# A gated layer whose matmuls use the two 64-row halves of the array side by side

## The chip, the cores and the metric

One core of a Trainium2 chip runs the whole kernel. The metric is the device time of one execution in microseconds (us). A difference is told from no change where it is over about 0.2%.

## The reference, cut to what matters

An mLSTM attention (4 batches, 8 heads, 768 positions, head size 40) gives 3072 rows of 320 numbers. Each row goes to one of eight experts (320 to 1024, relu, back to 320, times the row's routing weight). The last part is a gated layer, with 1536 hidden features:

```python
def _moe2_ref(x, w_gate, w_val, w_out):      # x [3072, 320]; w_gate, w_val [320, 1536]; w_out [1536, 320]
    gate = 1.0 / (1.0 + np.exp(-(x @ w_gate)))
    val = x @ w_val
    return (gate * val @ w_out).astype(np.float32)
```

## The kernel before

The kernel runs three stages after one another: attention, experts, gated layer. The order of instructions on each engine is the order in which the code issues them.

**Numbers in two parts.** Every operand of the experts and of the gated layer is held as a high and a low part (`split`, `f64_split`), both of the type float32r. A product is three matmuls into one bank of the accumulation memory: high by high, high by low, low by high.

**The gated layer** works on 6 groups of 512 rows (`NG`) by 12 blocks of 128 hidden features (`NF2`): 72 steps, numbered `t`, with `g = t // 12` and `f = t % 12`. In step `t`:

- `gated_l1(t)` takes two of the banks 0, 1, 2, 6 for gate and value and calls `l1_tile` (lines 922 to 926) for each. The 320 inputs are 128 + 128 + 64. The first two parts take three matmuls each. For the last 64, the weights' high and low parts stand under one another in one 128-row tile (`wgs`, `wvs`), the input stands in both halves of its own tile, and two matmuls give all four products. That is 8 matmuls of 512 columns for the gate and 8 for the value.
- then ScalarE takes the sigmoid (line 1527), VectorE multiplies (1528), ScalarE copies the high part `hh` (1530) and POOL subtracts for the low part `hl` (1532; in the last step VectorE does).
- `gated_l2(t - 2)` multiplies the features made two steps before by `w_out`: for each of 4 blocks of 128 rows three matmuls of 320 columns (lines 1544 to 1546), added up in banks 3, 4, 5, 7 over the 12 steps of a group.
- after the twelfth, `gated_out` copies the four banks (ScalarE line 1556, VectorE line 1558), and POOL issues an indirect DMA for each (1560).
- `piece()` prepares the next piece of weights: `f64_split` turns 64-bit inputs into the two parts with VectorE bit operations (lines 1076, 1079, 1082, then 1086, 1089 and the low part 1071) with one ScalarE relu (1085) in between and one ScalarE copy (1068). In the steps 0 to 11 these are the 12 pieces of `w_out`; those of `w_gate` and `w_val` are prepared during the experts, four of them for the last 64 rows, which write `wgs` and `wvs` with two low operations and two copies each. `defer` is a list of small operations on routing flags, of which eight are left when the gated layer starts; one of them is a matmul (line 1208).

In the experts, each hidden block has a low part `hl` made by VectorE (line 1015), which stands in VectorE's queue among the operations of the pieces, and which the matmuls of line 936 need.

**Elsewhere in the kernel**, the first attention tile multiplies 40-row operands that stand in the rows 0 to 39 and 64 to 103 (line 429; later tiles use all 128 rows), and line 476 writes 40-column results in two column halves.

Of the kernel before, what the change touches and what calls it, by code (L numbers as in the profile page):

```python
# [9 lines left out]
F32 = mybir.dt.float32  # L10
# [12 lines left out]
def kernel(  # L23
# [15 lines left out]
    nc = tc.nc  # L39
# [33 lines left out]
    def next_bank(banks, name):  # L73
        t = turn.get(banks, 0)
        turn[banks] = t + 1
        return bank(banks[t % len(banks)], name)
# [839 lines left out]
    def l1_tile(ps, ws, xt, f):  # L916

        hi, lo, st = ws
        h, l = xt
        fs = slice(f * P, (f + 1) * P)  # L920
        for kk in range(2):
            nc.tensor.matmul(ps, hi[:, kk, fs], h[:, kk], start=(kk == 0), stop=False)  # L922
            nc.tensor.matmul(ps, hi[:, kk, fs], l[:, kk], start=False, stop=False)  # L923
            nc.tensor.matmul(ps, lo[:, kk, fs], h[:, kk], start=False, stop=False)  # L924
        nc.tensor.matmul(ps, st[:, fs], h[:, 2], start=False, stop=False)  # L925
        nc.tensor.matmul(ps, st[:, fs], l[:, 2], start=False, stop=True)  # L926

    def ring(tag):
        return mw.tile([P, NM], F32R, tag=tag, name=tag, bufs=3)
# [481 lines left out]
    for nm in ("wg", "wv"):  # L1411
        glu[nm] = (
            gp.tile([P, 2, F2], F32R, name=nm + "h"),
            gp.tile([P, 2, F2], F32R, name=nm + "l"),
            gp.tile([P, F2], F32R, name=nm + "s"),
        )

    def whole(t):
        return t

    def glu_piece(nm, kk, c0, n):
        cs = slice(c0, c0 + n)
        if kk < 2:
            src = (w_gate if nm == "wg" else w_val)[:, cs].bitcast(I32)
            hi, lo, st = glu[nm]
            t = f64_load([(slice(0, P), src[kk * P:(kk + 1) * P])], n)
            return lambda: f64_split(t, n, [(whole, hi[:, kk, cs])], [(whole, lo[:, kk, cs])])

        halves = [slice(u * RM, (u + 1) * RM) for u in range(2)]
        t = f64_load(  # L1430
            [(r, w[:, cs].bitcast(I32)[2 * P:DM]) for r, w in zip(halves, (w_gate, w_val))], n
        )

        def parts(u):
            return [
                (lambda z, r=r: z[r], glu[m][2][halves[u], cs]) for r, m in zip(halves, ("wg", "wv"))
            ]

        return lambda: f64_split(t, n, parts(0), parts(1))


    todo = sorted(
# [75 lines left out]
        piece_load()  # L1518
    hs, os_ = {}, {}

    def gated_l1(t):
        g, f = t // NF2, t % NF2
        pg, pv = (next_bank((0, 1, 2, 6), nm) for nm in ("g_ps", "v_ps"))
        l1_tile(pg, glu["wg"], xg[g], f)
        l1_tile(pv, glu["wv"], xg[g], f)
        s = mw.tile([P, NM], F32, tag="sgm", bufs=2, name="sgm")
        nc.scalar.activation(out=s, in_=pg, func=AF.Sigmoid)  # L1527
        nc.vector.tensor_tensor(out=s, in0=pv, in1=s, op=ALU.mult)  # L1528
        gh, gl = ring("hh"), ring("hl")
        nc.scalar.copy(gh, s)  # L1530
        e = nc.gpsimd if t < last else nc.vector
        e.tensor_tensor(out=gl, in0=s, in1=gh, op=ALU.subtract)  # L1532
        hs[t] = (gh, gl)

    def gated_l2(t, js):
        g, f = t // NF2, t % NF2
        if f == 0:
            os_[g] = [bank(j, "o_ps") for j in (3, 4, 5, 7)]
        gh, gl = hs[t]
        wh, wl = wo[f]  # L1540
        for j in js:
            o = os_[g][j][:, 0:DM]
            ts_ = slice(j * P, (j + 1) * P)
            nc.tensor.matmul(o, gh[:, ts_], wh, start=(f == 0), stop=False)  # L1544
            nc.tensor.matmul(o, gh[:, ts_], wl, start=False, stop=False)  # L1545
            nc.tensor.matmul(o, gl[:, ts_], wh, start=False, stop=(f == NF2 - 1))  # L1546
# [19 lines left out]
            puts.append(put)  # L1566

    allj = range(G4)
    for t in range(NG * NF2):
        g, f = t // NF2, t % NF2  # L1570
        piece_due(t)
        gated_l1(t)
        if t >= 2:
            gated_l2(t - 2, allj)
            if (t - 2) % NF2 == NF2 - 1:
                gated_out(g - 1, allj)
        weave(defer[0:4], *piece())
        del defer[0:4]
        if g + 1 < NG and f in (4, 6, 8):
            group_x(g + 1, f // 2 - 2)  # L1580
    for j in allj:
# [188 lines left out]

    NSB = NE * NTILE

    def more_blocks(fp):
        gw = fp.tile([P, NTILE], F32, name="gw")
        for op in soft_ops(fp, gw, raw, ssq):
# [51 lines left out]
        with tc.For_i(0, NE, 1) as e:  # L1827
# [6 lines left out]
            with tc.If(high > low):  # L1834
# [7 lines left out]
                with tc.For_i(low, high, 1) as j:  # L1842
# [35 lines left out]
                    gl = fp.tile([P, NF2, P], F32R, name="fgl")  # L1878
                    for f in range(NF2):
                        pg = mm_ps("fg_ps")[:, 0:P]  # L1880
                        l1_tile(pg, glu["wg"], (yh, yl), f)
                        pv = mm_ps("fv_ps")[:, 0:P]
                        l1_tile(pv, glu["wv"], (yh, yl), f)
                        s = fp.tile([P, P], F32, tag="f_s", name="f_s")
                        nc.scalar.activation(out=s, in_=pg, func=AF.Sigmoid)
                        nc.vector.tensor_tensor(out=s, in0=pv, in1=s, op=ALU.mult)
                        split(gh[:, f], gl[:, f], s)
# [67 lines left out]
```

## Time and profile before

| | us |
|---|---|
| median of 3 runs | 780.74 (780.58 to 780.76) |
| the profiled execution | 783.19 |
| its span, from first to last instruction | 781.5 |
| TensorE matmul busy in the span | 742.0 (95%) |
| VectorE, ScalarE, POOL busy | 408.5, 339.4, 398.8 |

The span is what the trace covers; 1.7 us of the profiled execution lie around it. Busy times are shares of the whole span, and a busy TensorE means that some matmul was in flight, each of which lasts longer than the time to the next one's start. So the time that one matmul costs is read from starts, not from durations. The mean granted TensorE clock was 0.978.

### The profile page before, as it was taken

Reading aid. Unit: us, or ns where it says so; the run is one execution under the profiler, and the core shown is the slowest. Engines: PE = TensorE matmul, PEld = TensorE weight load, DVE = VectorE, ACT = ScalarE, POOL = GpSimd, SP = SyncE. Lnnn points to the kernel's source line nnn. Section 1 sums busy time; section 2 is a strip of 40 time slices with the busy share of each in tenths; the row PEclk is TensorE's granted clock in tenths of the full one; section 3 lists DMA queues with packets and bytes.
Section 4 is the critical chain, followed back from the end, with each engine's and each line's share of the span. In section 5 each row is a group of like instructions: output and inputs, shape, how many; then the busy total and the mean of one; then the engine's idle time right before and its main releaser. Section 6 shows DMA issues by size and latency. Waiting matters only on the chain.

```text
span 781.5 us, 13677 instructions
## 1 busy us (share of the span) xinstructions
PE 742.0 (95%) x5013; PEld 669.1 (86%) x5013; DVE 408.5 (52%) x858; ACT 339.4 (43%) x689; POOL 398.8 (51%) x449
## 2 busy tenths in 40 slices
PE   6789998999999999999999999999999999999995
PEld 5689997998778889998888888888888888888885
DVE  6888888777679889999676611111111111111111
ACT  5765554544866566765444422222222222222221
POOL 6677776647577668786323243342324324324222
PEclk9999999589999999999999999999999999999998
DMA  7555764444445566654022110000000000000001
GB/s 240 172 152 158 237 190 153 138 116 142 153 138 171 156 183 194 183 181 125 21 69 68 34 35 1 1 29 5 1 1 34 0 1 34 1 1 34 1 1 37
DMA packets 39846, 70.19 MB, mean 90 GB/s; under 512 B 4818, under 2 KB 28460, under 8 KB 39772
## 3 DMA queue, kind: packets, MB, share of 16 engines
q1 hardware_dynamic: 36764, 59.61, 25.5%
q0 software_dynamic: 3008, 9.64, 3.9%
q8 instruction: 41, 0.67, 0.3%
q14 instruction: 33, 0.27, 0.1%
HBM read 60.55 MB, written 8.68 MB: 89 GB/s over the span
## 4 chain that ended last, share of the span: by engine, by line
PE 61%; DVE 15%; issue 4%; ACT 1%; DMA 1%; POOL 1%; POOLq 0%; DVEq 0%; ACTq 0%
PE o_ps L1546 5%; PE o_ps L1545 5%; PE o_ps L1544 5%; PE g_ps L922 4%; PE g_ps L923 4%; PE g_ps L924 4%; PE v_ps L923 4%; PE v_ps L922 4%; PE v_ps L924 4%; DVE hl L1015 3%; PE v_ps L926 2%; PE v_ps L925 2%; PE g_ps L925 2%; PE g_ps L926 2%; DVE fa L1089 2%
## 5 line engine op out<-in xcount | busy, mean ns | idle before, releaser
L1532 POOL TENSOR_TENSOR hl<-sgm,hh 128x512 fp32r<-128x512 f32 x71 | 91.9, 1295 | 245.2 <-ACT hh L1530 245.1
L1528 DVE TENSOR_TENSOR sgm<-v_ps,sgm 128x512 f32<-128x512 f32 x72 | 49.8, 691 | 280.6 <-PE v_ps L926 275.2
L1530 ACT CAST hh<-sgm 128x512 fp32r<-128x512 f32 x72 | 44.7, 621 | 136.1 <-DVE sgm L1528 136.1
L1527 ACT ACTIVATE sgm<-g_ps 128x512 f32<-128x512 f32 x72 | 43.0, 597 | 122.6 <-PE g_ps L926 122.5
L1546 PE MATMUL o_ps<-wo,hl 128*128 128x320 f32 x288 | 89.0, 309 | 0.0
L1545 PE MATMUL o_ps<-wo,hh 128*128 128x320 f32 x288 | 88.9, 309 | 0.0
L1544 PE MATMUL o_ps<-wo,hh 128*128 128x320 f32 x288 | 88.6, 308 | 0.0
L429 PE MATMUL s_ps<-qk 128*128 128x128 f32 (+1 forms) x384 | 53.3, 300 | 5.9 <-DMA qk<-in_qkt_dram 5.3
L1544 PEld LDWEIGHTS o_ps<-wo,hh 128*128 128x128 f32 x288 | 54.1, 188 | 2.7
L1545 PEld LDWEIGHTS o_ps<-wo,hh 128*128 128x128 f32 x288 | 54.1, 188 | 2.7
L234 POOL TENSOR_TENSOR w2l<-w2raw,w2h 128x512 fp32r<-128x512 f32 x28 | 39.5, 1409 | 33.2 <-ACT w2h L232 20.9
L936 PE MATMUL y_ps<-hl,w2h 128*128 128x256 f32 (+7 forms) x144 | 49.7, 345 | 5.5 <-DVE hl L1015 5.3
L429 PEld LDWEIGHTS s_ps<-qk 128*128 128x128 f32 (+1 forms) x384 | 48.5, 209 | 7.2 <-DMA qk<-in_qkt_dram 4.8
L1546 PEld LDWEIGHTS o_ps<-wo,hl 128*128 128x128 f32 x288 | 54.1, 188 | 0.0
L223 POOL TENSOR_TENSOR w1l<-w1raw,w1h 128x512 fp32r<-128x512 f32 x32 | 46.2, 1443 | 10.2 <-ACT w1h L220 8.8
L922 PE MATMUL h_ps<-xh,w1h 128*128 128x256 f32 (+7 forms) x144 | 51.2, 356 | 0.0
L935 PE MATMUL y_ps<-hh,w2h 128*128 128x256 f32 (+7 forms) x144 | 50.2, 349 | 0.0
L924 PE MATMUL h_ps<-xh,w1l 128*128 128x256 f32 (+7 forms) x144 | 49.5, 344 | 0.0
L923 PE MATMUL h_ps<-xl,w1h 128*128 128x256 f32 (+7 forms) x144 | 49.4, 343 | 0.0
L1014 ACT ACTIVATE hh<-h_ps 128x256 fp32r<-128x256 f32 (+7 forms) x72 | 34.9, 487 | 32.7 <-PE h_ps L926 28.6
L937 PE MATMUL y_ps<-hh,w2l 128*128 128x256 f32 (+7 forms) x144 | 48.7, 339 | 0.0
L1015 DVE SCALAR_TENSOR_TENSOR hl<-h_ps,hh 128x256 fp32r<-128x256 f32 (+7 forms) x72 | 39.3, 548 | 13.0 <-ACT hh L1014 12.3
(334 smaller groups left out, 2086.4 us busy)
## 6 DMA issues: line engine op xcount, KB each, us to landing
kv<-in_kvo_dram SPq DMA_DIRECT2D x24, 484.0 KB
w2raw<-in_moe_w_dram SPq DMA_DIRECT2D x32, 320.0 KB
w1raw<-in_moe_w_dram SPq DMA_DIRECT2D x32, 256.0 KB
qk<-in_qkt_dram SPq DMA_DIRECT2D x48, 160.0 KB
xs<-x SPq DMA_DIRECT2D x24, 192.0 KB
w1raw<-in_moe_w_dram SPq DMA_DIRECT2D x64, 64.0 KB
raw<-in_moe_w_out_dram SPq DMA_DIRECT2D x12, 320.0 KB
raw<-in_moe_w_gate_dram SPq DMA_DIRECT2D x8, 384.0 KB
```

What stands on the lines that cost most here:

```text
L429: nc.tensor.matmul(pss[u][:, pr_ * L:(pr_ + 1) * L], qk[i % NQ][rows, 2 * u, pr_, :], qk[i % NQ][rows, 1, pr_, :], start=True, stop=True,)
L922: nc.tensor.matmul(ps, hi[:, kk, fs], h[:, kk], start=(kk == 0), stop=False)
L923: nc.tensor.matmul(ps, hi[:, kk, fs], l[:, kk], start=False, stop=False)
L924: nc.tensor.matmul(ps, lo[:, kk, fs], h[:, kk], start=False, stop=False)
L935: nc.tensor.matmul(ys[d], wh, hh, start=first, stop=False)
L936: nc.tensor.matmul(ys[d], wh, hl, start=False, stop=False)
L1015: nc.vector.scalar_tensor_tensor(out=h[f][1], in0=ps, scalar=0.0, in1=h[f][0], op0=ALU.max, op1=ALU.subtract)
L1528: nc.vector.tensor_tensor(out=s, in0=pv, in1=s, op=ALU.mult)
L1532: e.tensor_tensor(out=gl, in0=s, in1=gh, op=ALU.subtract)
L1544: nc.tensor.matmul(o, gh[:, ts_], wh, start=(f == 0), stop=False)
L1545: nc.tensor.matmul(o, gh[:, ts_], wl, start=False, stop=False)
L1546: nc.tensor.matmul(o, gl[:, ts_], wh, start=False, stop=(f == NF2 - 1))
```

## The change

The gated layer issues each matmul as two, on the rows 0 to 63 and 64 to 127 of the operands, and alternates them. In the first phase (`gated_a`) the upper half works on the gate and the lower half on the value: first the last 64 inputs, whose weights now stand as gate in rows 0 to 63 and value in rows 64 to 127 of two tiles `tails` (high, low), then the two blocks of 128, of which each half takes its own 64 rows. In the second phase (`gated_b`) the halves change banks and take the rows that are left. A one-element VectorE write (`seen`) waits for the last matmul of the first phase, and the first matmul of the second phase waits for that write. `gated_l2h` does the same with pairs of output blocks. The product of low by low parts, which the stacked tile had made for the last 64 inputs, is left out. On TensorE a step is `gated_a(t)`, `gated_l2h(t - 2, 0)`, `gated_b(t)`, `gated_l2h(t - 2, 1)`; at the start `gated_a(0)` and `gated_a(1)` come first. The steps 70 and 71 keep the old second layer. The pieces' operations are issued at other places of a step, and the low part `hl` after the output copies and DMAs.

```diff
...
+    tails = [gp.tile([P, F2], F32R, name="wt" + v) for v in "hl"]
...
     def glu_piece(nm, kk, c0, n):
         cs = slice(c0, c0 + n)
         if kk < 2:
             src = (w_gate if nm == "wg" else w_val)[:, cs].bitcast(I32)
-            hi, lo, st = glu[nm]
+            hi, lo = glu[nm]
             t = f64_load([(slice(0, P), src[kk * P:(kk + 1) * P])], n)
             return lambda: f64_split(t, n, [(whole, hi[:, kk, cs])], [(whole, lo[:, kk, cs])])
 
-        halves = [slice(u * RM, (u + 1) * RM) for u in range(2)]
         t = f64_load(
             [(r, w[:, cs].bitcast(I32)[2 * P:DM]) for r, w in zip(halves, (w_gate, w_val))], n
         )
-
-        def parts(u):
-            return [
-                (lambda z, r=r: z[r], glu[m][2][halves[u], cs]) for r, m in zip(halves, ("wg", "wv"))
-            ]
-
-        return lambda: f64_split(t, n, parts(0), parts(1))
+        return lambda: f64_split(t, n, [(whole, tails[0][:, cs])], [(whole, tails[1][:, cs])])
 
 
     todo = sorted(
...
+    gv = {}
+    gate_val = (glu["wg"], glu["wv"])
+
+    def products(rows, ps, w, x, kk, fs, start=False, stop=False):
+        (wh, wl), (h, l) = w, x
+        at = lambda z: z[rows, kk, fs] if len(z.shape) == 3 else z[rows, fs]
+        return [
+            lambda: nc.tensor.matmul(ps, at(wh), h[rows, kk], start=start, stop=False),
+            lambda: nc.tensor.matmul(ps, at(wh), l[rows, kk], start=False, stop=False),
+            lambda: nc.tensor.matmul(ps, at(wl), h[rows, kk], start=False, stop=stop),
+        ]
+
+    seen = const.tile([1, 1], F32, name="seen")
+    sync = mybir.DependencyInfo(mybir.DependencyClass.Sync, mybir.DependencyReason.DATA)
+    passed = {}
+
+    def woven(*chains):
+        return [op() for ops in zip(*chains) for op in ops]
+
+    def note(ins, key):
+
+        passed[key] = nc.vector.memset(seen, 0.0)
+        tc.add_manual_dep(passed[key].ins, ins.ins.name, sync, reason="these products are done")
+
+    def turn_rows(ins, key):
+
+        tc.add_manual_dep(ins.ins, passed.pop(key).ins.name, sync, reason="the other rows wrote the bank")
+
+    def gated_a(t):
         g, f = t // NF2, t % NF2
-        pg, pv = (next_bank((0, 1, 2, 6), nm) for nm in ("g_ps", "v_ps"))
-        l1_tile(pg, glu["wg"], xg[g], f)
-        l1_tile(pv, glu["wv"], xg[g], f)
+        fs = slice(f * P, (f + 1) * P)
+        gv[t] = [next_bank((0, 1, 2, 6), nm) for nm in ("g_ps", "v_ps")]
+        weave(*(products(r, ps, tails, xg[g], 2, fs, start=True) for r, ps in zip(halves, gv[t])))
+        for kk in range(2):
+            ins = woven(*(products(r, ps, w, xg[g], kk, fs) for r, ps, w in zip(halves, gv[t], gate_val)))
+        note(ins[-1], "l1")
+
+    def gated_b(t):
+        g, f = t // NF2, t % NF2
+        fs = slice(f * P, (f + 1) * P)
+        for kk in range(2):
+            ins = woven(*(
+                products(r, ps, w, xg[g], kk, fs, stop=(kk == 1))
+                for r, ps, w in zip(halves, gv[t][::-1], gate_val[::-1])
+            ))
+            if kk == 0 and "l1" in passed:
+                turn_rows(ins[0], "l1")
+        pg, pv = gv.pop(t)
         s = mw.tile([P, NM], F32, tag="sgm", bufs=2, name="sgm")
         nc.scalar.activation(out=s, in_=pg, func=AF.Sigmoid)
         nc.vector.tensor_tensor(out=s, in0=pv, in1=s, op=ALU.mult)
+        return s
+
+    def gated_h(t, s):
         gh, gl = ring("hh"), ring("hl")
         nc.scalar.copy(gh, s)
         e = nc.gpsimd if t < last else nc.vector
         e.tensor_tensor(out=gl, in0=s, in1=gh, op=ALU.subtract)
         hs[t] = (gh, gl)
+
+    def gated_l2h(t, phase):
+        g, f = t // NF2, t % NF2
+        swap = (f + phase) % 2
+        begin, end = f == 0 and phase == 0, f == NF2 - 1 and phase == 1
+        if begin:
+            os_[g] = [bank(j, "o_ps") for j in (3, 4, 5, 7)]
+        gh, gl = hs[t]
+        wh, wl = wo[f]
+
+        def three(rows, j):
+            o = os_[g][j][:, 0:DM]
+            ts_ = slice(j * P, (j + 1) * P)
+            return [
+                lambda: nc.tensor.matmul(o, gh[rows, ts_], wh[rows], start=begin, stop=False),
+                lambda: nc.tensor.matmul(o, gh[rows, ts_], wl[rows], start=False, stop=False),
+                lambda: nc.tensor.matmul(o, gl[rows, ts_], wh[rows], start=False, stop=end),
+            ]
+
+        for j in (0, 2):
+            ins = woven(*(three(halves[u], j + (u ^ swap)) for u in range(2)))
+            if phase and j == 0:
+                turn_rows(ins[0], "l2")
+        if not phase:
+            note(ins[-1], "l2")
 
     def gated_l2(t, js):
         g, f = t // NF2, t % NF2
@@ -1566,16 +1632,31 @@
             puts.append(put)
 
     allj = range(G4)
+    rest = ([], [])
     for t in range(NG * NF2):
         g, f = t // NF2, t % NF2
         piece_due(t)
-        gated_l1(t)
-        if t >= 2:
-            gated_l2(t - 2, allj)
+        if t < 2:
+            if t == 0:
+                gated_a(0)
+                gated_a(1)
+            weave(rest[0])
+            s = gated_b(t)
+        else:
+            gated_a(t)
+            gated_l2h(t - 2, 0)
+            weave(rest[0])
+            s = gated_b(t)
+            gated_l2h(t - 2, 1)
             if (t - 2) % NF2 == NF2 - 1:
                 gated_out(g - 1, allj)
-        weave(defer[0:4], *piece())
-        del defer[0:4]
+        weave(rest[1])
+        a, b, *rest = piece()
+        weave(a)
+        gated_h(t, s)
+        weave(b)
+        weave(defer[0:3])
+        del defer[0:3]
         if g + 1 < NG and f in (4, 6, 8):
             group_x(g + 1, f // 2 - 2)
     for j in allj:
...
```

(A fall-back path for rows that overflow an expert, which does not run with these inputs, reads the new tiles in the same way.)

## Rows read from the trace of the kernel before

**Rows 1.** stretches of time: busy time of each engine, mean granted clock, DMA

```profile
383.30:767.40 384.10, 384.10 (x1983) 337.34 (x1982) 89.63 (x163) 110.70 (x195) 131.12 (x106) 1.00 0.06 18
```

**Rows 2.** timeline of TensorE in the gated layer: start, length, what

```profile
605.23 0.30 PE L1544 MATMUL o_ps<-wo,hh 128*128 128x320 f32 x1
...
606.99 0.39 PE L922 MATMUL g_ps<-xh,wgh 128*128 128x512 f32 x1
...
610.64 0.30 PE L1544 MATMUL o_ps<-wo,hh 128*128 128x320 f32 x1
```

**Rows 3.** timeline of all engines, the same steps

```profile
603.68 0.60 ACT L1527 ACTIVATE sgm<-g_ps 128x512 f32<-128x512 f32 x1 [1.71 <-PE g_ps L926]
...
605.50 0.69 DVE L1528 TENSOR_TENSOR sgm<-v_ps,sgm 128x512 f32<-128x512 f32 x1 [4.71 <-PE v_ps L926]
...
606.23 0.62 ACT L1530 CAST hh<-sgm 128x512 fp32r<-128x512 f32 x1 [1.95 <-DVE sgm L1528]
...
606.93 1.29 POOL L1532 TENSOR_TENSOR hl<-sgm,hh 128x512 fp32r<-128x512 f32 x1 [2.87 <-ACT hh L1530]
```

**Rows 4.** timeline of half-array and full-array matmuls (x: how many merged)

```profile
5.25 0.28 PEld L429 LDWEIGHTS s_ps<-qk 40*128 40x128 f32 x1 [0.53 <-DMA qk<-in_qkt_dram]
...
5.25 0.29 PEld L429 LDWEIGHTS s_ps<-qk 40*128 40x128 f32 x2 [0.53 <-DMA qk<-in_qkt_dram]
...
5.25 2.07 PE L429 MATMUL s_ps<-qk 40*128 40x128 f32 x14 [0.24 <-DMA qk<-in_qkt_dram]
...
9.92 3.75 PE L429 MATMUL s_ps<-qk 128*128 128x128 f32 x16 [0.85 <-DMA qk<-in_qkt_dram]
...
101.87 0.24 PE L476 MATMUL u_ps<-vw,kv 128*40 128x41 f32 x2
```

**Rows 5.** timeline of weight loads for matmuls of eight columns, and these

```profile
104.08 0.64 PEld L541 LDWEIGHTS l_ps<-enT,xt 128*128 128x128 f32 x5
...
104.19 0.62 PE L541 MATMUL l_ps<-enT,xt 128*128 128x8 f32 x5
```

**Rows 6.** timeline of VectorE where the gated layer starts

```profile
387.25 0.69 DVE L1528 TENSOR_TENSOR sgm<-v_ps,sgm 128x512 f32<-128x512 f32 x1 [2.17 <-PE fl_ps L1208]
...
389.10 1.21 DVE L1086 SCALAR_TENSOR_TENSOR fb<-raw,fa 128x320 int32<-128x320 int32 x1 [0.92 <-ACT fa L1085]
...
390.24 0.14 DVE L1236 TENSOR_SCALAR fl<-fl 128x1 f32<-128x1 f32 x1
...
390.54 0.31 DVE L1089 TENSOR_SCALAR fa<-fb 128x320 int32<-128x320 int32 x1
...
390.84 0.47 DVE L1082 SCALAR_TENSOR_TENSOR fc<-raw,fc 128x320 int32<-128x320 int32 x1
...
391.35 0.49 DVE L1071 SCALAR_TENSOR_TENSOR wo<-fc,fa 128x320 fp32r<-128x320 int32 x1
```

**Rows 7.** timeline of all engines at the end

```profile
769.08 0.69 DVE L1532 TENSOR_TENSOR hl<-sgm,hh 128x512 fp32r<-128x512 f32 x1 [0.69 <-ACT hh L1530]
...
769.83 0.19 PEld L1546 LDWEIGHTS o_ps<-wo,hl 128*128 128x128 f32 x1
...
770.98 1.00 POOL L1560 DMA_INDIRECT out_dram<-ot,perm  x1 [5.97 <-ACT ot L1556]
...
774.86 0.98 POOL L1560 DMA_INDIRECT out_dram<-ot,perm  x1 [0.30 <-issue]
```

**Rows 8.** timeline in the sixth expert, all engines

```profile
332.17 0.70 DVE L1071 SCALAR_TENSOR_TENSOR wgs<-fc,fa 64x384 fp32r<-64x384 int32 x1
...
332.89 1.54 DVE L1071 SCALAR_TENSOR_TENSOR wvs<-fc,fa 64x384 fp32r<-64x384 int32 x1
...
335.07 0.44 PE L936 MATMUL y_ps<-hl,w2h 128*128 128x384 f32 x1 [1.18 <-DVE hl L1015]
```

**Rows 9.** who waited, 374 to 378 us: total, times, longest

```profile
PE y_ps L936 <- DVE hl L1015: 1.2, 1, 1.2
```

**Rows 10.** the chain of work that ended last, in order of time

```profile
375.10 1.55 DVE wvs L1071
```

More of the change, by code (lines that the diff above doesn't have):

```diff
@@ L1414 @@
             gp.tile([P, 2, F2], F32R, name=nm + "l"),
-            gp.tile([P, F2], F32R, name=nm + "s"),
         )
+    tails = [gp.tile([P, F2], F32R, name="wt" + v) for v in "hl"]
     def whole(t):
         return t
+    halves = [slice(u * RM, (u + 1) * RM) for u in range(2)]
     def glu_piece(nm, kk, c0, n):
@@ L1519 @@
     hs, os_ = {}, {}
-    def gated_l1(t):
-        g, f = t // NF2, t % NF2
-        pg, pv = (next_bank((0, 1, 2, 6), nm) for nm in ("g_ps", "v_ps"))
-        l1_tile(pg, glu["wg"], xg[g], f)
-        l1_tile(pv, glu["wv"], xg[g], f)
+    gv = {}
[19 more added lines that the diff above has]
+    def gated_a(t):
+        g, f = t // NF2, t % NF2
+        fs = slice(f * P, (f + 1) * P)
[15 more added lines that the diff above has]
+        pg, pv = gv.pop(t)
         s = mw.tile([P, NM], F32, tag="sgm", bufs=2, name="sgm")
@@ L1771, with l1_any @@
     NSB = NE * NTILE
+    def l1_any(ps, u, x, f):
+        fs = slice(f * P, (f + 1) * P)
+        for rows, w, kk in (
+            (slice(0, P), gate_val[u], 0), (slice(0, P), gate_val[u], 1), (halves[u], tails, 2)
+        ):
+            weave(products(rows, ps, w, x, kk, fs, start=(kk == 0), stop=(kk == 2)))
     def more_blocks(fp):
@@ L1880, in more_blocks @@
                         pg = mm_ps("fg_ps")[:, 0:P]
-                        l1_tile(pg, glu["wg"], (yh, yl), f)
+                        l1_any(pg, 0, (yh, yl), f)
                         pv = mm_ps("fv_ps")[:, 0:P]
-                        l1_tile(pv, glu["wv"], (yh, yl), f)
+                        l1_any(pv, 1, (yh, yl), f)
                         s = fp.tile([P, P], F32, tag="f_s", name="f_s")
```

## The prediction, made before the changed kernel had run

> **What bounds the kernel now.** I read the stretches of time first. From the first gated matmul to the last of step 71, 383.3 to 767.4, TensorE has a matmul in flight for all of 384.10 us; VectorE is busy for 89.63, ScalarE for 110.70, POOL for 131.12 [rows 1]. So in this half of the kernel only TensorE's own pace counts. The timeline gives that pace by starts: the 16 first-layer matmuls of a step run from 606.99 to 610.64, 3.65 us or 0.228 each; the 12 of the second layer from 605.23 to 606.99, 1.76 us or 0.1465 each; a step takes 5.41 [rows 2]. Check: 72 × 3.65 + 69 × 1.76 = 384.2. No step waits: 0.27 us after the last value matmul's slot ends (605.23) VectorE multiplies, and ScalarE and POOL follow long before the result is needed two steps later [rows 3]. What an edit saves on TensorE here is therefore saved in the end, as long as no new wait takes it back.
>
> **The change, part by part.** The question that decides is whether two half-array matmuls run side by side.
>
> *Are pairs free?* The trace has such pairs. At the start of the attention two weight loads of 40-row operands, one in each half, lie within 0.29 us, where one alone takes 0.28; 14 half-array matmuls take 2.07 us where, a little later, 16 full ones of the same 128 columns take 3.75 [rows 4]. At the full array's pace of 3.75/16 = 0.234, seven pairs would take 1.64 and 14 singles 3.28; the rest of the 2.07 is the first load, which nothing hides. Pairs of column halves behave alike (two in 0.24) [rows 4]. These are plain float32 in 128 columns, not float32r in 512, so the bounds are: nothing for the second half, or the last digit's 0.01 per pair. I take nothing, since in a chain each half follows its own predecessor and only the first offset shows.
>
> *First layer.* 16 full matmuls become 18 + 12 halves, 15 pairs: one slot of 0.228 less in each of 72 steps. −16.4 us.
>
> *Second layer.* 12 matmuls become 12 pairs of the same 320 columns: 0.
>
> *The phase writes.* 142 one-element VectorE writes. A one-element operation took 0.14 [rows 6]; VectorE starts 0.27 after the slot of the matmul it waits for [rows 2, 3], and TensorE's load follows a VectorE end by 0.06 (769.77 to 769.83) [rows 7]. The gate is open 0.27 + 0.14 + 0.06 = 0.47 after the first phase. Meanwhile TensorE does six second-layer pairs, 0.88; and six first-layer pairs, 1.37, ahead of the second layer's gate. So 0, with 0.4 to spare. VectorE is not in the way: after the last second phase it has multiplied by 0.27 + 0.60 + 0.69 = 1.6, the three first operations of a weight piece (0.47 the longest [rows 6]) end by 2.7, and the write is due only at 0.88 + 9 × 0.228 + 0.27 = 3.2. Without the cover each step would lose the 0.47.
>
> *The start.* Here there is no cover. `gated_a(0)` and `gated_a(1)` run back to back and `gated_b(0)` waits at once: 0.47 and a load of 0.19, 0.65. Then VectorE's queue holds, after E (the end of `gated_b(0)`): the multiply from 0.9 (0.27 + 0.60 and a step), the rest of piece 0 with its relu wait, until about 2.8 when operation 1086 can start (1.85 after the multiply's start: 389.10 − 387.25), then 1.2 + 0.3 + 0.5, to 4.8; only then the multiply of step 1 (0.69), the first part of piece 1 (about 1.0), small ones (0.2) and the write that opens `gated_b(2)`: E + 6.7. TensorE's own work to there is 1.37 + 2.05 + 0.88 = 4.3. So 2.4 of waiting, 3.1 with the first. Step 3 has room again. Bounds 0.7 (VectorE never late) and 4. +3.1.
>
> *The end.* Half of the second layer's call in step 71 (0.88) now stands ahead of the last first-layer matmul; in the old order all of it stood behind. So that matmul ends 0.88 later than the first-layer saving alone would have it: +0.9. The sigmoid used to run beside the value matmuls; now both banks are ready together, and the last chain (0.27, sigmoid 0.60, multiply 0.69, copy 0.62, subtract 0.69, steps of 0.04 to 0.06) needs 3.0 to the last kind of matmul; it was 2.4 (767.4 to 769.83 [rows 1, 7]), a time that the second layer filled. +0.6, and it passes on, since POOL's output DMAs are a chain of 1.29 each from the first to the last: (774.86 − 770.98)/3 [rows 7]. In all other steps the late sigmoid is free: the features are needed after 8 us and are there after 3.6.
>
> *Moved past POOL's queue.* `hl` now stands behind the four output DMAs of a group: 4 × 1.29 from about 1.9, then its own 1.29 [rows 3, 7], ready 8.4 after `gated_b`; needed at 8.3. With a few switches between full and half array, +0.3 in all, bounds 0 and 2.
>
> *The weight pieces.* Each of the four pieces for the last 64 rows loses one VectorE low operation and one ScalarE copy. Two of them are where TensorE waits for VectorE: operations of 0.70 and 1.54 stand in front of `hl`, and matmul 936 idles 1.18 [rows 8]; the same at 375.10, which is on the chain that ended last, with a wait of 1.2 [rows 9, 10]. Taking away 0.70 to 1.54 at both frees 1.4 to 2.4 and a little at the others; bounds 0 and 3.3. −2.5.
>
> Sum: −16.4 + 3.1 + 0.9 + 0.6 + 0.3 − 2.5 = −14.0. The profiled execution (783.19, span 781.5, 1.7 around it) would be 769.2. The runs' median is 780.74, 2.45 below the profiled one; the same sum there gives **766.7 us**.
>
> A rule that speaks against the change: the Trainium skill, TensorEngine Tiling (Array Packing), section Instruction Overhead, says that each matmul has about 60 cycles of overhead. As a toll on each of the 26 extra matmuls of a step that would be, as an estimate, 25 ns × 26 × 72 = 47 us, and 814 in place of 766.7. The two loads in 0.29 and two matmuls in 0.24 [rows 4] do not show such a toll; no run here shows it for float32r.
>
> **The rivals.**
>
> *The second half has a price.* If each pair costs 0.005 to 0.01 more, 15 × 72 + 12 × 70 = 1920 pairs cost 10 to 19 us: 776 to 786, by the middle (0.0075) 781, no change. For: the loads' 0.29 against 0.28 [rows 4]. Against: in a chain the offset need not add up. This is what the skill's rule would do here, as far as rows can price it.
>
> *The halves' weight loads queue up* (the other side). Five loads of 128 columns for matmuls of 8 columns take 0.64, so (0.64 − 0.19)/4 = 0.112 each, load after load [rows 5]. Two in turn are 0.224: hidden under 0.228, but not under the second layer's 0.1465. 840 × 0.078 = +65, 832 us. It decides as soon as such a pair costs 0.017 more, 14/840. Against: two loads in 0.29 [rows 4].
>
> *The gate opens late in every step*, because VectorE or the way there and back is slower than 0.88. At 1.2 us: 72 × 0.4 = +29, 796. Against: the 0.47.
>
> *Pairs are better than free.* From 320 to 512 columns a slot grows by 0.081, 0.42 ns per column, so of 0.228 only 0.216 is streaming and 0.012 is fixed. If one half's fixed part hides behind the other's streaming, 1920 × 0.012 = −22: 745; half of it 756. Nothing in the rows shows it.
>
> **How the numbers follow.** Side by side at the old slots 0.58 (own range 763 to 771, from the bounds of start, weight pieces and POOL); a price per pair 0.14; better than free 0.10; loads in turn 0.06; late gate 0.07; others, such as halves that do not overlap at all in float32r, 0.05. The range reaches to half of "better than free" on the one side and the middle of the price on the other: 755 to 781. Measurement tells 0.2% (1.6 us) from no change. Faster: 0.58 + 0.10 + 0.08 of the price case + 0.01; the rest of the price case is mostly no change; loads, gate and others are slower. Faster 0.77, same 0.07, slower 0.16.
>
> **What would show it.** Right: in a middle step pairs start 0.228 apart (first layer) and 0.1465 (second), the two of a pair within 0.01, weight loads of both halves side by side, a step of 5.18, TensorE without gaps from step 3 on, and about 3 us of gaps in steps 0 to 2; no waits of 1.2 at the two weight pieces. Wrong: second-layer pairs 0.16 to 0.22 apart (price, or loads in turn); a gap ahead of each first matmul of `gated_b` (late gate); slots under 0.22 (better than free).

## The result, and the profile after

The changed kernel takes 774.73 us (median of 5 runs, 770.93 to 775.29), the kernel before, beside it, 780.74 (780.16 to 781.24): ratio 0.9912, 95% interval 0.9888 to 0.9936. Forecast was 766.7. So it is faster, by 6.0 us where 14.0 were expected. The profiled execution took 770.93, 12.3 less than the profiled one of before. Which of the 12.3 belong to the change is read stage by stage.

The stretches of time of the kernel after: routing, experts (to the first gated matmul), gated layer to the end of the span, and the middle of it (columns: stretch, length, busy time and count of PE, PEld, DVE, ACT, POOL, granted clock, DMA share, GB/s).

```profile
147.95:190.70 42.75, 40.89 (x328) 40.25 (x327) 34.60 (x92) 21.00 (x50) 24.85 (x27) 0.89 0.47 141
190.70:377.30 186.60, 182.90 (x971) 165.38 (x967) 157.40 (x260) 119.97 (x243) 132.24 (x126) 1.00 0.54 160
377.30:769.10 391.80, 379.79 (x3866) 328.49 (x3865) 97.00 (x309) 111.60 (x198) 135.91 (x110) 0.99 0.06 20
392.00:754.00 362.00, 362.00 (x3732) 315.02 (x3732) 85.88 (x281) 103.65 (x184) 129.13 (x104) 1.00 0.06 19
```

The same stretches of the kernel before:

```profile
147.93:192.95 45.02, 42.32 (x328) 41.45 (x327) 34.58 (x92) 20.83 (x50) 24.90 (x27) 0.86 0.46 134
192.95:383.33 190.38, 183.35 (x971) 165.52 (x968) 162.65 (x264) 122.06 (x247) 133.35 (x126) 1.00 0.53 156
383.33:781.48 398.15, 389.55 (x2019) 342.49 (x2017) 91.97 (x167) 112.17 (x198) 135.07 (x110) 0.99 0.06 19
```

The experts give 3.8 us and the gated layer 6.35, together 10.1. The other 2.3 lie in the routing, which the change doesn't touch and where the granted clock was 0.89 in place of 0.86: over the 17 profiles of this case the routing takes 42.0 to 45.0 us and the attention 147.5 to 151.2, whichever gated layer runs. The experts take 189.8 to 190.9 in the four profiles with the old gated layer and 186.6 to 187.8 in the thirteen with the new one or a variant of it, so 3.2 on average. From 392 to 754 TensorE has a matmul in flight all the time, as before [rows 1].

The timeline of TensorE in one gated step after (start, length, what; x2: the pair merged), to be set against [rows 2]:

```profile
605.43 0.30 PE L1589 MATMUL o_ps<-wo,hh 64*128 64x320 f32 x2
...
606.31 0.39 PE L1523 MATMUL v_ps<-xh,wvh 64*128 64x512 f32 x1
606.31 0.39 PE L1523 MATMUL g_ps<-xh,wgh 64*128 64x512 f32 x1
606.54 0.39 PE L1524 MATMUL v_ps<-xl,wvh 64*128 64x512 f32 x1
...
607.70 0.31 PE L1589 MATMUL o_ps<-wo,hh 64*128 64x320 f32 x2
...
608.58 0.39 PE L1523 MATMUL g_ps<-xh,wth 64*128 64x512 f32 x1
...
610.67 0.30 PE L1589 MATMUL o_ps<-wo,hh 64*128 64x320 f32 x2
```

The two of a pair start within 0.01 us. Six second-layer pairs take 0.88 (605.43 to 606.31): 0.1465 each, the old slot of one full matmul, so the second half is free. But the 15 first-layer pairs take 1.39 + 2.09 = 3.48, or 0.232 each, where the old slot was 0.228. The step is 5.24, not 5.18.

The waits at the start and at the end (timeline; in brackets the idle time and what ended it):

```profile
381.95 0.49 PE L1523 MATMUL v_ps<-xg,wvh 64*128 64x512 f32 x1 [0.18 <-DVE seen L1537]
...
388.04 0.42 PE L1589 MATMUL o_ps<-wo,hh 64*128 64x320 f32 x2 [0.62 <-ACT wo L1068]
...
389.13 0.30 PE L1591 MATMUL o_ps<-wo,hl 64*128 64x320 f32 x2
391.26 0.50 PE L1523 MATMUL v_ps<-xg,wvh 64*128 64x512 f32 x1 [1.82 <-DVE seen L1537]
...
756.72 0.42 PE L1610 MATMUL o_ps<-wo,hh 128*128 128x320 f32 x1 [0.62 <-ACT hh L1571]
...
757.44 0.42 PE L1612 MATMUL o_ps<-wo,hl 128*128 128x320 f32 x1 [0.16 <-DVE hl L1573]
```

By starts these cost more than the idle time: 389.13 to 391.26 is 2.13 where a slot is 0.147, so 1.98 are lost and not 1.82.

How long TensorE waited for `hl` in the experts: first after, then before, each from 193 us to the gated layer (total, times, longest):

```profile
PE y_ps L936 <- DVE hl L1015: 1.4, 2, 1.0
```

```profile
PE y_ps L936 <- DVE hl L1015: 3.8, 4, 1.2
```

### The profile page after: what moved, and what is told of

It is laid out like the page before. It is cut to its first block, busy times and chain, and to the rows that moved or that the text cites. A ratio compares the mean times of both kernels' runs of the same rounds, so it can differ in the third digit from the quotient of the medians.

```text
span 769.1 us, 17570 instructions
## 1 busy us (share of the span) xinstructions
PE 730.6 (95%) x6861; PEld 653.9 (85%) x6861; DVE 408.4 (53%) x996; ACT 336.9 (44%) x685; POOL 398.7 (52%) x449
## 5 line engine op out<-in xcount | busy, mean ns | idle before, releaser
L1591 PE MATMUL o_ps<-wo,hl 64*128 64x320 f32 x560 | 86.6, 306 | 0.0
L1589 PE MATMUL o_ps<-wo,hh 64*128 64x320 f32 x560 | 86.0, 304 | 0.6 <-ACT wo L1068 0.6
L1590 PE MATMUL o_ps<-wo,hh 64*128 64x320 f32 x560 | 86.4, 305 | 0.0
L1589 PEld LDWEIGHTS o_ps<-wo,hh 64*128 64x128 f32 x560 | 52.6, 184 | 7.4 <-ACT wo L1068 1.1
L1523 PE MATMUL v_ps<-xg,wvh 64*128 64x512 f32 x144 | 56.7, 394 | 2.0 <-DVE seen L1537 2.0
L1590 PEld LDWEIGHTS o_ps<-wo,hh 64*128 64x128 f32 x560 | 52.5, 184 | 6.1 <-DVE wo L1071 0.2
L1523 PE MATMUL g_ps<-xg,wgh 64*128 64x512 f32 x144 | 56.7, 394 | 0.0
L1524 PE MATMUL g_ps<-xl,wgh 64*128 64x512 f32 x144 | 56.4, 392 | 0.0
L1524 PE MATMUL v_ps<-xl,wvh 64*128 64x512 f32 x144 | 56.4, 392 | 0.0
L1524 PE MATMUL v_ps<-xg,wvh 64*128 64x512 f32 x144 | 56.4, 392 | 0.0
L1524 PE MATMUL g_ps<-xg,wgh 64*128 64x512 f32 x144 | 56.4, 392 | 0.0
L1523 PE MATMUL g_ps<-xh,wgh 64*128 64x512 f32 x144 | 56.3, 391 | 0.0
L1523 PE MATMUL v_ps<-xh,wvh 64*128 64x512 f32 x144 | 56.3, 391 | 0.0
L1525 PE MATMUL g_ps<-xg,wgl 64*128 64x512 f32 x144 | 56.2, 390 | 0.0
```

The lines of the kernel that those rows point to most:

```text
L1523: lambda: nc.tensor.matmul(ps, at(wh), h[rows, kk], start=start, stop=False),
L1524: lambda: nc.tensor.matmul(ps, at(wh), l[rows, kk], start=False, stop=False),
L1525: lambda: nc.tensor.matmul(ps, at(wl), h[rows, kk], start=False, stop=stop),
L1589: lambda: nc.tensor.matmul(o, gh[rows, ts_], wh[rows], start=begin, stop=False),
L1590: lambda: nc.tensor.matmul(o, gh[rows, ts_], wl[rows], start=False, stop=False),
L1591: lambda: nc.tensor.matmul(o, gl[rows, ts_], wh[rows], start=False, stop=end),
```

## The experiments

Ratios are against runs of the kernel before on the same chip. "Step" is the time between like starts in the middle of the gated layer; "gated stage" runs from its first matmul to the end of the span.

| run | what | median us | ratio, 95% | step | gated stage |
|---|---|---|---|---|---|
| | before | 780.74 | | 5.41 | 398.15 |
| | after | 774.73 | 0.9912 (0.9888 to 0.9936) | 5.24 | 391.80 |
| e1 | after, unchanged | 773.78 | 0.9896 (0.9865 to 0.9927) | 5.24 | 391.8 |
| e2 | full array at the start | 769.55 | 0.9840 (0.9813 to 0.9867) | 5.24 | 389.3 |
| e3 | halves for the tails alone | 796.89 | 1.0196 (1.0164 to 1.0229) | 5.64 | 415.3 |
| e4 | halves in one stretch | 771.72 | 0.9875 (0.9850 to 0.9899) | 5.25 | 391.0 |
| e5 | after, no tile moved | 772.68 | 0.9876 (0.9847 to 0.9904) | 5.20 | 388.97 |
| e6 | before, tiles moved by 32 bytes | 788.68 | 1.0070 (1.0044 to 1.0095) | 5.49 | 404.20 |
| e8 | e2, e4 and e5 together | 766.43 | 0.9783 (0.9756 to 0.9811) | 5.18 | 384.56 |

### Start, order, halves

Theory A put the lost 8 us on the clock at the gated start, rival B on the routing stage. Theory C and rival D are about the longer slots.

*e1*, no edit. 

> The changed kernel once more, unchanged. Its profiled execution took 770.93 us, but four of its five runs took 773.4 to 775.3, with a lower mean granted clock (0.974 to 0.978 against 0.982). Theory A: the ordinary runs have one or two more stretches at the lower of the two clock levels at the start of the gated layer, where TensorE waits about 3 us in three gaps; the trace of an ordinary run shows a low granted clock between 377 and 395 us. Rival B: the stretches vary in the routing stage (147 to 172 us), in whichever kernel, and the gated layer is at full clock in each run; then runs of this kernel and of the kernel before scatter alike. Median expected 774 to 775 under both.

In its profile (771.96) the granted clock is 1.00 from 377 to 395 us and the gated stage takes 391.8 again, so A is not seen here; "The gap at the start" below comes back to it. The kernel before scatters too, from 778.57 to 785.19 beside it, and the profiles show the routing and the attention vary with either gated layer. That is B's scatter; it does not belong to the change.

*e2*: the steps 0 and 1 take the blocks of 128 inputs with the full array, and only the tails in halves (the definition of `gated_full`, which does that, is left out).

```diff
-            if t == 0:
-                gated_a(0)
-                gated_a(1)
             weave(rest[0])
-            s = gated_b(t)
+            s = gated_full(t)
```

> Steps 0 and 1 use full-array matmuls for the first two input blocks and half pairs for the last 64 inputs only, one step after the other, so that the first phase write is not waited for at once. Theory A (gaps at the start cost clock): the three gaps (0.35 + 0.79 + 1.98 us and smaller ones) go, and the lower clock after them; 774.7 to about 769. Rival B (clock varies elsewhere): only the gaps go, less two switches between full and half array per step; 774.7 to 772 or 773. If VectorE's queue still opens the gate of step 2 late: no change.

The gated stage is 2.45 us shorter and TensorE's waits at the start are down to 0.8. So the halves' phases at the start cost what the forecast said, in kind and about in size. The median falls by more, 4.2 us; which of A and B the rest belongs to, this run does not tell.

*e3*: that form in every step, with the old second layer and no phase writes (shortened: the branch for the first two steps goes too).

```diff
-            gated_a(t)
-            gated_l2h(t - 2, 0)
-            weave(rest[0])
-            s = gated_b(t)
-            gated_l2h(t - 2, 1)
+        weave(rest[0])
+        s = gated_full(t)
+        if t >= 2:
+            gated_l2(t - 2, allj)
```

> Half pairs for the last 64 inputs alone; the first two input blocks and the second layer use the full array in every step; no phase writes. 15 slots of 512 columns and 12 of 320 in a step, as in the changed kernel, but two switches between full and half array in each step. If a switch costs nothing, a step takes 5.19 us and the kernel about 769 (no gaps at the start). If a switch waits until the array is empty, some 0.1 to 0.2 us each, 72 x 2 x 0.1 to 0.2 = 14 to 29 us more: 783 to 798, slower than before. Halves throughout would then be what makes the saving possible.

It has the same 15 slots and is slower than before. The timeline of TensorE where it goes from the full array to halves and back:

```profile
603.63 0.40 PE L1524 MATMUL v_ps<-xl,wvh 128*128 128x512 f32 x1
603.87 0.39 PE L1525 MATMUL v_ps<-xh,wvl 128*128 128x512 f32 x1
604.19 0.18 PEld L1523 LDWEIGHTS g_ps<-xh,wth 64*128 64x128 f32 x1 [0.36 <-issue]
604.19 0.50 PE L1523 MATMUL g_ps<-xh,wth 64*128 64x512 f32 x1
...
604.53 0.39 PE L1524 MATMUL g_ps<-xl,wth 64*128 64x512 f32 x1
604.76 0.39 PE L1525 MATMUL g_ps<-xh,wtl 64*128 64x512 f32 x1
...
605.09 0.42 PE L1610 MATMUL o_ps<-wo,hh 128*128 128x320 f32 x1
605.34 0.31 PE L1611 MATMUL o_ps<-wo,hh 128*128 128x320 f32 x1
```

The slots around the switches are 0.32, 0.34, 0.33 and 0.25 in place of 0.233, 0.233, 0.233 and 0.147: 0.4 us a step, 29 us in 72. The first weight load behind a switch starts together with its matmul (both 604.19). The Trainium skill, TensorEngine Tiling (Array Packing), Key Properties, says that a change of tiling mode drains TensorE; the trace agrees in the longer slots and the late load, but does not show the array empty, since the modelled ends overlap the next start. This is why the change has to use halves throughout. And the full-array slots ahead of the switch average 0.233 here too (603.63 to 603.87 is one of them): the pairs are not what made the slots longer, so D falls in its first form.

*e4*: `gated_b(t)` and `gated_a(t + 1)` directly behind one another, and the two halves of the second layer too, so that a step goes from 320 to 512 columns once and not twice (shortened: the first step of a group and the last step differ).

```diff
-            gated_a(t)
-            gated_l2h(t - 2, 0)
-            weave(rest[0])
-            s = gated_b(t)
-            gated_l2h(t - 2, 1)
+        gated_l2h(t - 3, 1)
+        gated_l2h(t - 2, 0)
+        weave(rest[0])
+        s = gated_b(t)
+        gated_a(t + 1)
```

> Same matmuls, other order: the second phase of a step and the first phase of the next stand together, and so do the two halves of the second layer, so that TensorE goes from 320-column to 512-column matmuls once in a step and not twice. Theory C: the first six or so slots of 512 columns after such a change are longer (231 to 236 ns against 227), so the twelve second-layer pairs in a row followed by 15 first-layer pairs pay it once: a step of 5.19 to 5.20 in place of 5.24, and 72 x 0.045 = 3 us less; late slots in the block are 227 ns. Rival D: each half pair costs 3 to 6 ns more than a full matmul wherever it stands: step 5.24 and no change.

The last three slots of a stretch of 15, and the start of the second layer behind them:

```profile
603.47 0.39 PE L1523 MATMUL g_ps<-xh,wgh 64*128 64x512 f32 x1
...
604.16 0.30 PE L1589 MATMUL o_ps<-wo,hh 64*128 64x320 f32 x2
```

They take 0.69. The slots alternate between 0.231 and 0.235 up to the end of the stretch, and the step stays at 5.25. As it stood then, C fell as well.

### Where the operands lie

The order in which the program lays out its tiles showed one thing by which all these kernels differ from the one before: the new one-word tile `seen` takes 32 bytes ahead of the buffers of `w_out`, and the tokens `xg`, the hidden blocks and `w_out` all start 32 bytes later. The gated weights, laid out from the other end, stay. In the kernel before, tokens and gated weights start at the same place modulo 512 bytes. Theory E is that these addresses set the slot, rival F that they don't.

*e5* takes the word from a tile that is there; *e6* gives the kernel before the same shift and nothing else.

```diff
-    dum = const.tile([P, 1], F32, name="dum")
+    dum2 = const.tile([P, 2], F32, name="dum")
+    dum = dum2[:, 0:1]
...
-    seen = const.tile([1, 1], F32, name="seen")
+    seen = dum2[0:1, 1:2]
```

```diff
-    dum = const.tile([P, 1], F32, name="dum")
+    dum = const.tile([P, 9], F32, name="dum")[:, 0:1]
```

> The word that the phase writes go to is the second word of a tile that is there already, so that no operand lies elsewhere in SBUF than in the kernel before (in the changed kernel the new one-word tile takes 32 bytes ahead of the weights, and all tiles behind it start 32 bytes later). Theory E (addresses): the slot of 512 columns of the first layer depends on where its operands start: here it is back at 226.7 ns for most of a step, as in the kernel before, where it is 231 to 236 ns in the changed kernel; 5 ns x 15 slots x 72 steps = 5 us less, 768 to 770 us. Rival F (order): the slot is set by what runs around it and not by addresses: slots stay at 231 to 236 ns and the time at that of the changed kernel, 773 to 775 us.

> The kernel before with one constant tile 32 bytes longer, so that the weights, the tokens and the hidden blocks start 32 bytes later, as in the changed kernel; nothing else differs. Theory E: all first-layer slots at 231 to 236 ns instead of 226.7 for 11 of 16; 5 ns x 11 x 72 = 4 us more, 784 to 786 us, with a step of 5.46 to 5.48 us instead of 5.41. Rival F: no change, 781 us, step 5.41 us.

The timeline of TensorE of e5, from the seventh pair of a stretch of nine:

```profile
605.11 0.39 PE L1524 MATMUL v_ps<-xh,wvh 64*128 64x512 f32 x1
605.33 0.39 PE L1525 MATMUL g_ps<-xl,wgh 64*128 64x512 f32 x1
...
605.56 0.39 PE L1526 MATMUL g_ps<-xh,wgl 64*128 64x512 f32 x1
605.56 0.39 PE L1526 MATMUL v_ps<-xh,wvl 64*128 64x512 f32 x1
605.79 0.30 PE L1590 MATMUL o_ps<-wo,hh 64*128 64x320 f32 x2
```

and of e6, one whole step:

```profile
605.02 0.30 PE L1544 MATMUL o_ps<-wo,hh 128*128 128x320 f32 x1
...
608.18 0.40 PE L925 MATMUL g_ps<-xh,wgs 128*128 128x512 f32 x1
...
608.88 0.39 PE L923 MATMUL v_ps<-xl,wvh 128*128 128x512 f32 x1
...
610.51 0.30 PE L1544 MATMUL o_ps<-wo,hh 128*128 128x320 f32 x1
```

In the kernel before, the last three first-layer slots of a step start here and end at 605.23 [rows 2], 0.68 later:

```profile
604.55 0.39 PE L924 MATMUL v_ps<-xh,wvl 128*128 128x512 f32 x1
```

Three slots of e5 take 0.68 as well (605.11 to 605.79), 0.227 each; in e6 three take 0.70, 0.233. The kernel before loses 0.08 a step and 0.7% of its time by 32 unused bytes: theory E holds, F falls. The time of e5 alone would not have told: its median, 772.68, lies between the two ranges, and its ratio's interval overlaps e1's. In e5 the step drops to 5.20 and the gated stage by 2.8 us, less than the 5 expected: the first five slots behind each switch from 320 to 512 columns are 0.228 to 0.236 here and in the kernel before alike, whatever the addresses, and the change makes that switch twice a step.

*e7*: a shift of 64 bytes.

```diff
-    seen = const.tile([1, 1], F32, name="seen")
+    seen = const.tile([1, 9], F32, name="seen")[0:1, 0:1]
```

> The changed kernel with the new tile 64 bytes long instead of 32. Theory E, if it is the place within 64 bytes that counts: as without a shift, slots at 226.7 ns, gated stage some 5 us shorter than the 391.8 of the changed kernel. If the place within 128 bytes or more counts, or under Rival F: slots at 231 to 236 ns.

Neither: the first-layer slots don't settle (0.226 to 0.236 in turn) and average 0.2313, where e5 has 0.2300 and the changed kernel 0.2327. The second layer's are a little shorter (0.1447 in place of 0.1458), so the step is 5.207, almost that of no shift. The one execution took 773.1.

*e8* puts the edits of e2, e4 and e5 together. 

> The changed kernel without the shift, with the first two steps in full-array matmuls and half pairs only for the last block of rows, and from then on the two first-layer halves and the two second-layer halves each in one stretch. Theory E: the sum of what each gave alone, 774.2 - 4.4 (start) - 5 (addresses) - 1 to 2 (one stretch each) = 763 to 766 us. Rival F: 768 to 770 us.

The time is 766.43, ratio 0.9783, close to the sum. The step, from two like starts of its timeline:

```profile
599.77 0.39 PE L1524 MATMUL g_ps<-xh,wth 64*128 64x512 f32 x1
...
604.96 0.39 PE L1524 MATMUL g_ps<-xh,wth 64*128 64x512 f32 x1
```

Over 60 steps it is 5.18: what the forecast had for the change itself. With the tiles in place, one stretch does help: the step is 0.02 shorter than in e5, 1.4 us in 72. So C was half right and e4 could not show it, because there the slots never settled.

### Which operand

One execution each; the kernel before took 781.31 on this chip. E1 says that the place of the tokens by itself counts, E2 that it is their place against the weights.

*e9* puts 32 unused bytes ahead of the tokens and hidden blocks (`w_out` stays), *e10* behind the gated weights, which start 32 bytes earlier by it, both in the kernel before (the first line is e9's, the second e10's).

```diff
+    wp.tile([P, 8], F32, tag="gap", name="gap")
...
+    gp.tile([P, 8], F32, name="gap")
```

> The kernel before with 32 unused bytes ahead of the token blocks alone: the streamed operand of the first layer (xg) and the tiles of the hidden blocks start 32 bytes later, the weights of both layers stay. Theory E1 (where the streamed operand lies, by itself): slots at 231 to 236 ns throughout, as in the shifted kernel before, step 5.46 to 5.48 us. Theory E2 (how the streamed operand lies against the weights that are loaded beside it): the same here, since the two no longer match. If it is the second layer's weights (wo) or the expert stage that count: slots settle at 226.7 ns, step 5.41 us.

> The kernel before with the gated weights starting 32 bytes earlier and the token blocks where they were. E1: slots settle at 226.7 ns, step 5.41 us, 781 us. E2: slots stay at 230 to 236 ns, step 5.46 to 5.48 us.

*e11* gives the changed kernel a shift of 128 bytes, *e12* one of 480 for the tokens and of -32 for the weights (e11's first line, then e12's two).

```diff
+    seen = const.tile([1, 32], F32, name="seen")[0:1, 0:1]
...
+    gp.tile([P, 8], F32, name="gap")
...
+    seen = const.tile([1, 120], F32, name="seen")[0:1, 0:1]
```

> The changed kernel with a shift of 128 bytes in place of 32: tokens and weights start at the same place within 128 bytes, as in the kernel before, but not within 256. If the place within 128 bytes decides, under E1 and E2: slots settle at 226 to 227 ns from the sixth behind a switch on, as without a shift, gated stage 389 us. If more of the address counts: some 231 to 236 ns throughout, 391.8 us.

> The changed kernel with the tokens shifted by 480 bytes and the gated weights by -32: both start at byte 448 of a line of 512, where both started at 480 in the kernel before. E1: the place has changed, slots at 230 to 236 ns throughout, gated stage 391.8 us. E2: tokens and weights match again, so slots settle at 226 to 227 ns from the sixth on, gated stage 389 us.

| run | tokens against weights (bytes, modulo 512) | step | time |
|---|---|---|---|
| before | 0 | 5.41 | 781.31 |
| e9 | 32 (tokens moved) | 5.49 | 788.60 |
| e10 | 32 (weights moved) | 5.49 | 788.07 |
| e11 | 128 | 5.25 | 774.24 |
| e12 | 0 (both at another place) | 5.20 | 770.28 |

The timelines of e10, a whole step, of e11, one pair, and of e12, three slots:

```profile
603.92 0.39 PE L922 MATMUL g_ps<-xh,wgh 128*128 128x512 f32 x1
...
609.40 0.39 PE L922 MATMUL g_ps<-xh,wgh 128*128 128x512 f32 x1
```

```profile
604.05 0.39 PE L1523 MATMUL g_ps<-xh,wgh 64*128 64x512 f32 x1
604.08 0.39 PE L1523 MATMUL v_ps<-xh,wvh 64*128 64x512 f32 x1
```

```profile
605.32 0.39 PE L1525 MATMUL v_ps<-xh,wvh 64*128 64x512 f32 x1
...
606.00 0.31 PE L1591 MATMUL o_ps<-wo,hh 64*128 64x320 f32 x2
```

Moving the weights alone does the same as moving the tokens alone, and moving both together brings the short slots back (0.68 for three). So E2 holds against E1: what counts is how the streamed tokens lie against the gated weights. Whether it is the load of the next weights beside the stream that matters, no run tells. 128 bytes are not enough of a match; there the second matmul of a pair starts 0.03 behind the first.

### The gap at the start

The profiles of e11 and e12 had a stretch of low clock behind the gated start (0.83 over 390 to 400 us in both), that of the kernel after had none. A2 says that the gap brings the clock down, its rival that the clock falls now and then whatever the gap. *e13* holds the gate of step 2 back with 50 more writes, *e14* does so in e8 in four steps in the middle, *e15* is the kernel after again.

```diff
-    def note(ins, key):
+    def note(ins, key, hold=0):
+        for _ in range(hold):
+            k = nc.vector.memset(seen, 0.0)
+            tc.add_manual_dep(k.ins, ins.ins.name, sync, reason="a late gate")
...
-        note(ins[-1], "l1")
+        note(ins[-1], "l1", hold=50 if t in (2,) else 0)
```

> The changed kernel with the gate of step 2 opened later: 50 more one-word VectorE writes of 59 ns each stand between the last matmul of that step's first phase and the write that opens it, so TensorE waits some 5 us there instead of 2. Theory A2 (a gap at the gated start brings TensorE's clock down for a stretch, in some executions or in all): a stretch of granted clock 0.5 within some 20 us behind the gap, and a time more than 3 us above the changed kernel's, 778 to 782 us. Rival (the clock falls in the gated stage now and then whatever the gap): granted clock 1.00 there as in most profiles, only the gap's 3 us more, 776 to 778 us.

> The best version so far (no shift, first two steps in full-array matmuls, halves in one stretch each) with the same 50 writes in four steps in the middle, 20, 32, 44 and 56, each of which opens a gap of some 2 us in a stage that had none. A2: a stretch of granted clock 0.5 behind one or more of the gaps; 4 x 2 us for the gaps and up to 1.7 us for each such stretch, 776 us or more. Rival: granted clock 1.00 throughout the stage, 774 to 775 us.

> The changed kernel unchanged, for one more profile on the same chip. A2: where its time is near its median of 774 us rather than near the 771 of its first profile, the trace has a stretch of granted clock 0.5 behind the gaps of the gated start, as the profiles of the two shifted versions had. Rival: the difference lies in the routing stage (a longer stretch of 0.5 there).

The stretches of time behind the gap, of the kernel after, of e15, of e13 and, behind one of the four gaps, of e14 (columns as above, the clock third from the end):

```profile
395.00:400.00 5.00, 5.00 (x54) 4.28 (x52) 3.80 (x11) 1.69 (x5) 1.42 (x1) 1.00 0.21 67
```

```profile
395.00:400.00 5.00, 5.00 (x38) 4.28 (x38) 3.18 (x8) 2.03 (x4) 1.21 (x1) 0.68 0.22 69
```

```profile
400.00:405.00 5.00, 5.00 (x40) 4.34 (x38) 2.80 (x6) 2.03 (x4) 1.42 (x1) 0.70 0.16 56
```

```profile
620.00:625.00 5.00, 0.94 (x14) 0.67 (x10) 2.60 (x44) 0.00 (x0) 0.59 (x1) 1.00 0.01 2
625.00:630.00 5.00, 4.98 (x30) 3.98 (x32) 0.75 (x2) 1.74 (x3) 0.72 (x1) 0.66 0.00 0
```

and the timeline of TensorE of e15 in that stretch:

```profile
394.19 0.49 PE L1523 MATMUL v_ps<-xg,wvh 64*128 64x512 f32 x1 [1.83 <-DVE seen L1537]
...
395.15 0.63 PE L1523 MATMUL v_ps<-xg,wvh 64*128 64x512 f32 x1
...
395.58 0.63 PE L1524 MATMUL v_ps<-xg,wvh 64*128 64x512 f32 x1
...
396.01 0.63 PE L1525 MATMUL v_ps<-xg,wvl 64*128 64x512 f32 x1
```

Behind the wait of 1.83 the slots are 0.43, near the pace of the lower clock (1.2 GHz). In 5 us at full clock there are 54 matmuls, here 38. e15's gated stage is 393.25 against 391.80. In e14, which without the gaps (e8) has clock 1.00 there, the clock falls behind all four; TensorE waits 16.3 us in sum, and the gated stage takes 410.29 where e8's takes 384.56, so 25.7 more. The median rises by 24.2, to 790.58, on another chip. e13 has a gap of 7.6 us, longer than meant, since 50 writes took 5.7 us and not 3; its time (780.05) fits both theories, and its clock row is one profile that speaks for A2. Four falls of four in e14 decide. So a gap can cost more than its length. It does so in some executions only: of seven profiles with the kernel after's gap of 2 us, three show it (e11, e12, e15). And it is not the whole of the 4.4 us by which e15 (775.32) lies above the first profile: 1.45 are in the gated stage, 2.94 in the attention (150.89 against 147.95, clock 0.91 against 0.95). There the rival is right that it lies outside the gated stage, but not that it is the routing, which took 42.8 in both.

## Why the prediction missed, point by point

**The step that failed is the first-layer term**: "one slot of 0.228 less in each of 72 steps. −16.4 us". The slot did go, but the 15 that stayed grew from 0.228 to 0.232. The term took the average of 16 slots for the price of each, as if it did not depend on where a slot stands or on where its operands lie. The step shrank by 0.17, not 0.228: 72 × 0.17 = 12, so 4.3 us are missing. Of these, 0.04 a step or 2.9 us are the 32 bytes that the one-word tile took (5.24 against e5's 5.20), and 0.02 or 1.4 us the second switch between 512 and 320 columns (5.20 against e8's 5.18). Rows 2 give the average of a step as a constant; slot by slot the same trace shows 0.228 to 0.236 for the first five and 0.227 for the rest, and that it was not constant was there to be asked about.

**Pairs are free**: right, within 0.01. None of the price, the queueing loads, the late gate or the "better than free" came: second-layer slots are the old 0.1465, and with the tiles in place and one stretch (e8) the first-layer ones average 0.228 again. Two readings behind it were off without harm: by starts the attention's pairs are 0.21 apart, as its full matmuls are, and not 0.234, which divides a whole length; and a gate that opens at 1.2 would be 0.32 late and not 0.4, so 790 and not 796. The 60 cycles for each matmul that the Trainium skill, TensorEngine Tiling (Array Packing), states under Instruction Overhead are no toll here: with 26 matmuls more the step became shorter.

**The phase writes cost nothing in the middle**: right. They take 59 ns each, not 0.14, and from 392 to 754 TensorE never waits.

**The start, +3.1**: right in length, in part by luck. By starts the waits are 0.35, 0.79 and 1.98, in sum 3.1. The forecast had 0.65 and 2.4 for the two gates, and the middle wait, for a copy of `w_out`, it did not have. Priced too low all the same, since such a gap can bring the clock down, for 1.45 us in e15.

**The end, +0.9 and +0.6**: right. From the last first-layer matmul to the last matmul it takes 5.99 where it took 5.36. About 1 us more than the terms went, at the start, into slots that are some 0.1 to 0.25 longer behind each wait and behind the matmul of line 1208. For such slots and for POOL's queue, which held nothing up from 392 to 754, the forecast had 0.3.

**The weight pieces, −2.5**: the wait for `hl` fell by 2.4 (3.8 to 1.4), as said; the stretch as a whole gave 3.8, since TensorE's other waits there, all for VectorE, fell by 1.0 too (3.0 to 2.0). No run takes this part alone.

With −12.0 for −16.4 the profile's sum is −12.0 + 3.1 + 0.9 + 0.6 + 1 − 3.8 = −10.2, and the stages show −10.1. That the profiled execution, 770.93, came near its 769.2 is luck: the routing gave 2.3. That the medians differ by only 6.0, and by 7.9 on the next chip, is put down to attention, routing and the low clock behind the gap. The medians of e2, e4 and e8, without that gap or with a shorter one, gain what the experts and the gated stage gain in their profiles, within 0.5 us; those of the kernel after, e1 and e5, which have it, gain 4.1, 2.0 and 1.4 less. That speaks for the gap, but one fall is worth 1.45 and not 4.1, and how much falls on each in the unprofiled runs stays open.

## What to carry to other kernels

Two 64-row halves on two banks run at the pace of one full matmul, so what counts is the number of slots; but each change between full and half array cost about 0.2 us here, so use one form throughout. After an edit, read the slots of the matmuls that did not change: a new tile of one word moved every operand laid out behind it and cost 2.9 us, more than the two gates at the start (2.3). Where TensorE is the bound, price a gap above its length (in e15 2 us cost 1.45 more), and close gaps in the start-up steps first (e2 gave 4.2 us on the median for an edit of two steps).

## What the runs showed of the hardware

- Two 64-row matmuls on different rows and banks start within 0.01 us of each other and take the slot of one full matmul: 0.1465 for 320 columns, 0.228 on average for 512 (e8).
- The slot of a 512-column float32r matmul depends on where its streamed operand starts against the weights: once settled, 0.227 when both start at the same place modulo 512 bytes, 0.231 to 0.235 with 32 bytes between them. 64 bytes cost little (5.207 a step against 5.20); with 128, a step takes 5.25 and a pair's second matmul is 0.03 late. Other distances (256 among them) were not tried, and why it is so stays open.
- Even with matching addresses, the first five slots behind 320-column matmuls are 0.228 to 0.236. The cause was not found.
- A change between full and half array made two slots longer by about 0.1 each (e3).
- Behind a wait of 1.8 us at the gated start the granted clock fell in three profiles of seven (0.68 over 5 us in e15), behind four waits of 4.1 us in all four cases (0.66 to 0.71 over 5 us in e14).
